# Sketch attention and mixture of experts on one core: k's load in front of S2's, a shorter chain of word operations, shared copies, 1e-6 by a product, and q pieces moved by one place

## The chip, the cores and the metric

One core of a Trainium2 chip. The metric is the device time of one execution in microseconds (us). The profiled span is some 1.8 us shorter than the device time of the same execution (489.55 and 491.35 us in the kernel before). In the views, PE is TensorE's matmuls, PEld its weight loads, DVE VectorE, ACT ScalarE, POOL GpSimd and SP SyncE; a pass is one matmul instruction, and a unit is the group of tokens whose queries are handled together.

## The reference, cut to what matters

```python
# q, k, v: (4, 4, 1088, 32); S1, S2: (8, 32) float64
def phi(x):                        # 64 features: products of two 8-wide projections
    a = einsum('rd,bhsd->bhsr', S1, x); b = einsum('rd,bhsd->bhsr', S2, x)
    return einsum('bhsi,bhsj->bhsij', a, b).reshape(..., 64)
kv  = einsum('bhsf,bhsd->bhfd', phi(k), v);  z = sum(phi(k), axis=s)
num = einsum('bhsf,bhfd->bhsd', phi(q), kv)
den = einsum('bhsf,bhf->bhs',  phi(q), z)[..., None] + 1e-06
x   = (num / den) as (4352, 128)
for e in range(4):                 # dense mixture of experts, D = 128, F = 1024
    out += p[:, e:e+1] * (relu(x @ w1[e]) @ w2[e])
```

S1 and S2 arrive as float64, two 32-bit words for each number. The kernel builds float32 from the words with integer operations on VectorE.

## The kernel before

The opening: loads on SyncE's and ACT's queues, warm-up matmuls, and the words of S. In the traces VectorE's operations of the opening start in the order of the program: in the changed kernel k had landed at 4.55 us, but its transpose, which stands behind the words, started at 6.58.

```python
s_raw = ...                                   # 16 x 64 int32: S1 over S2
for i, (eng, src) in enumerate(((nc.scalar, S1), (nc.sync, S2))):
    eng.dma_start(s_raw[R * i : R * i + R, :], src.bitcast(I32))
...
load_rows(k, 0, "kn")                         # 544 KB, SyncE's queue
load_rows(q, 0, "qn", slice(0, P))            # 64 KB
vn[0] = load_v(0)
...                                           # dp, ends, rest of q, w1 and w2 of each expert
keep_warm(10)                                 # 10 bf16 matmuls of 512 columns on zeros
# --- cut: thirteen word operations, a product, a transpose into s_T on VectorE ---
for h in range(H):
    nc.scalar.copy(<sk block h>, <s_T>)       # 4 on ACT
for i in range(3):
    nc.gpsimd.tensor_copy(<sp i>, <s_T>)      # 3 on POOL
for h in range(H):
    nc.gpsimd.tensor_copy(<sr block h>, <sp>) # 4 on POOL
# start(): transpose k (kT) and q; k projections kT x sk on TensorE; q's by sr;
#   products kp, qp; sums f over tokens; kvz; den and num; 1/den; xT; MoE begins
```

In the first unit 1e-6 is added on VectorE between den's transpose and the reciprocal. The later units run as small pieces between the MoE steps, one piece at each `yield`:

```python
def queries(b, c, n):
    qT = query_turn(b, c, n)                  # transpose on VectorE
    yield; yield; yield
    both(qc, sq, qT)                          # q projection on TensorE
    ...                                       # shuffles, sums, products qp on VectorE
    yield; yield
    yield from attend(...)                    # den products on TensorE, divide, transpose

def attend(...):
    for t in range(T[0]):                     # token tiles
        for p in range(2):                    # feature pairs
            for _ in range(2): on_side(nd[...], qp[p][:, at:at+64], kvx[b][:, p, :])
```

Of the kernel before, what the change touches and what calls it, by code (L numbers as in the profile page):

```python
# [8 lines left out]
F32 = mybir.dt.float32  # L9
# [14 lines left out]
def kernel(  # L24
# [58 lines left out]
    def psum(pool, tag):  # L83
        return pool.tile([P, 512], F32, tag=tag, name=tag)


    def load_rows(src, b, name, part=slice(0, S)):

        d = kn if name == "kn" else qn
        if b not in d:  # L90
            d[b] = lpool.tile([P, S], F32, tag=name, bufs=2, name=name)
        c, n = part.start, part.stop - part.start
        nc.sync.dma_start(d[b][:, part], bass.AP(src.tensor, src.offset + b * H * S * D + c, [[G * D, P], [1, n]]))
# [21 lines left out]
        load_rows(q, b, "qn")  # L115

    s_raw = cpool.tile([R2, 2 * D], I32, name="s_raw")
    for i, (eng, src) in enumerate(((nc.scalar, S1), (nc.sync, S2))):
        eng.dma_start(s_raw[R * i : R * i + R, :], src.bitcast(I32))  # L119
    w1_sb = cpool.tile([P, E, F], F32, name="w1_sb")  # L120
# [5 lines left out]
    def load_w2(e):  # L126
        nc.sync.dma_start(w2_sb[:, e], w2[e].rearrange("(f p) d -> p f d", p=P))

    load_rows(k, 0, "kn")
    load_rows(q, 0, "qn", slice(0, P))  # L130
    vn[0] = load_v(0)

# [36 lines left out]
    for h in range(H):  # L169
        nc.gpsimd.memset(own2[32 * h : 32 * h + 32, h % 2 : h % 2 + 1], 1.0)  # L170

    def keep_warm(n):

        for _ in range(n):
            wp = psum(ps_h, "h")
            nc.tensor.matmul(wp[:, :], warm[:, 0:P], warm[:, :], start=True, stop=True)  # L176

    keep_warm(10)


    turn = [0]
# [17 lines left out]
    def bits(out, in0, s1, op0, s2=None, op1=ALU.bypass):  # L199
        nc.vector.tensor_scalar(out=out, in0=in0, scalar1=s1, scalar2=s2, op0=op0, op1=op1)  # L200

    def either(out, a, b):
        nc.vector.tensor_tensor(out=out, in0=a, in1=b, op=ALU.bitwise_or)

    low = _ap(s_raw, 0, R2, 0, [[2, D]])
    high = _ap(s_raw, 0, R2, 1, [[2, D]])
# [5 lines left out]
    nc.vector.memset(s_hl[:, :], 0.0)  # L212
    bits(s_f[:, hi], high, 1, shl, 21, shr)
    bits(s_m[:, lo], high, 31, shr, 31, shl)

    bits(s_e[:, hi], s_f[:, hi], float(127 - 1023), ALU.add, 0.0, ALU.max)
    bits(s_e[:, lo], s_f[:, hi], float(127 - 1023 - 52), ALU.add, 0.0, ALU.max)
    bits(s_x[:, hi], high, 12, shl, 9, shr)
    bits(s_x[:, lo], low, 29, shr)
    bits(s_n[:, hi], s_e[:, hi], 1.0, ALU.min)  # L220
    bits(s_n[:, lo], low, 3, shl, 3, shr)
    bits(s_f[:, :], s_e[:, :], 255.0, ALU.min)
    either(s_x[:, hi], s_x[:, hi], s_x[:, lo])
    bits(s_e[:, :], s_f[:, :], 23, shl)
    either(s_m[:, hi], s_x[:, hi], s_m[:, lo])
    either(s_f[:, :], s_e[:, :], s_m[:, :])
    nc.vector.tensor_tensor(out=s_hl[0:R2, :], in0=s_n[:, :], in1=s_f[:, :].bitcast(F32), op=ALU.mult)
    nc.vector.transpose(s_T[:, :], s_hl[:, :])




    for h in range(H):
        nc.scalar.copy(_ap(sk, 32 * h, 32, R2 * h, [[HP, 2], [1, R2]]), _ap(s_T, 0, 32, 0, [[D, 2], [1, R2]]))
    for i in range(3):
        nc.gpsimd.tensor_copy(
            _ap(sp, 0, 32, HP * i, [[32, 2], [R, 4], [1, R]]),
            _ap(s_T, 0, 32, 4 * (i - 1) if i else R, [[D, 2]] + ([[1, 4], [0, R]] if i else [[0, 4], [1, R]])),
        )
    for h in range(H):  # L240
        nc.gpsimd.tensor_copy(
            _ap(sr, 32 * h, 32, 32 * h, [[P, 6], [1, 32]]), _ap(sp, 0, 32, 0, [[32, 6], [1, 32]])
        )
    mask_lo = [R2 + l % R2 for l in range(32)]
    mask_b = [R + l % R for l in range(32)]
    mask_a = [[4 * x + l // R for l in range(32)] for x in range(2)]
# [210 lines left out]
    def attend_first(b, c, n, qp):  # L457


        nd = [psum(ps_n, "den"), psum(ps_n, "num")]  # L460
        for i in range(2):
            for _ in range(2):
                on_side(
                    lambda s: nd[i][half[s], 0:n],
                    lambda s: kvzs[b][:, s, 1 - i, :],
                    lambda s: qp[s][:, 0:n],
                    start=True,
                    stop=True,
                )
        yield  # L470
        dT = apool.tile([P, UNITS[0][1]], F32, tag="dT", name="dT")
        nc.vector.transpose(dT[:, 0:n], nd[0][:, 0:n])
        yield
        rc = apool.tile([P, QW // 32], F32, tag="rc", name="rc")
        nc.vector.tensor_scalar(
            out=rc[:, 0 : n // 32], in0=_ap(dT, 0, P, 0, [[32, n // 32]]), scalar1=1e-6, scalar2=1.0, op0=ALU.add, op1=ALU.mult
        )
        nc.vector.reciprocal(rc[:, 0 : n // 32], rc[:, 0 : n // 32])
        rb = apool.tile([P, UNITS[0][1]], F32, tag="rb", name="rb")
        nc.vector.transpose(  # L480
            _ap(rb, 0, P, 0, [[32, n // 32], [1, 32]]), _ap(rc, 0, P, 0, [[1, n // 32], [0, 32]])
        )
        yield

        order = [[1, 4], [4, 32]] if c == 0 else [[32, n // 32], [1, 32]]
        nc.vector.tensor_tensor(  # L486
            out=_ap(xT, 0, P, c, order),
            in0=nd[1][:, 0:n].rearrange("p (g j) -> p g j", j=32),
            in1=rb[:, 0:n].rearrange("p (g j) -> p g j", j=32),
            op=ALU.mult,  # L490
        )
        have[0] += n
        yield

    def attend(b, c, n, qp):



        nd = [psum(ps_n, "den"), psum(ps_n, "num")]
        W = H * (D + 1)  # L500
        tiles = 0
        laid = []
        for c0, m in unit_parts(b, c, n):
            T = blocks(m)
            for t in range(T[0]):
                for p in range(2):
                    for _ in range(2):

                        at = c0 + P * t + (HP * turn[0] if t < T[turn[0]] else 0)
                        i, k = divmod(tiles + t, 3)  # L510
                        on_side(
                            lambda s: nd[i][half[s], W * k + W // 2 * p : W * k + W // 2 * (p + 1)],
                            lambda s: qp[p][:, at : at + HP],
                            lambda s: kvx[b][:, p, :],
                            start=True,
                            stop=True,
                        )
            laid.append((c0, T, tiles))
            tiles += T[0]
        yield  # L520
        banks = [(i, 3 * i, min(tiles, 3 * i + 3)) for i in range((tiles + 2) // 3)]
        rc = apool.tile([P, QW // 32], F32, tag="rc", name="rc")
        for i, t0, t1 in banks:
            nc.vector.tensor_scalar(
                out=rc[:, H * t0 : H * t1],
                in0=_ap(nd[i], 0, P, D, [[D + 1, H * (t1 - t0)]]),
                scalar1=1e-6, scalar2=1.0, op0=ALU.add, op1=ALU.mult,
            )
        nc.vector.reciprocal(rc[:, 0 : H * tiles], rc[:, 0 : H * tiles])
        yield  # L530
        xs = apool.tile([P, QW], F32, tag="qa", name="xs")
        for i, t0, t1 in banks:
            nc.vector.tensor_tensor(
                out=_ap(xs, 0, P, P * t0, [[D, H * (t1 - t0)], [1, D]]),
                in0=_ap(nd[i], 0, P, 0, [[D + 1, H * (t1 - t0)], [1, D]]),
                in1=_ap(rc, 0, P, H * t0, [[1, H * (t1 - t0)], [0, D]]),
                op=ALU.mult,
            )
        yield
        y = apool.tile([P, QW], F32, tag="y", name="y")  # L540
        for c0, T, t0 in laid:
            nc.vector.transpose(
                _ap(y, 0, P, P * t0, [[32, T[0]], [32 * T[0], H], [1, 32]]),
                _ap(xs, 0, P, P * t0, [[P, T[0]], [D, H], [1, D]]),
            )
            m = 64 * sum(T)
            base = xd.offset + P * (S * b + c + c0)
            for a in range(4):
                run = 32 * T[a // 2]
                nc.sync.dma_start(  # L550
                    bass.AP(
                        xd.tensor,
                        base + a // 2 * 64 * T[0] + a % 2 * run,
                        [[m, 32], [32 * m, H], [1, run]],
                    ),
                    _ap(y, 32 * a, 32, P * t0, [[32 * T[0], H], [1, run]]),
                )
            nc.sync.dma_start(
                xT[:, S * b + c + c0 : S * b + c + c0 + m],
                bass.AP(xd.tensor, base, [[m, P], [1, m]]),  # L560
            )
        have[0] += n
        yield

    def queries(b, c, n):
        qT = query_turn(b, c, n)
        yield
        yield
        yield
        qc = psum(ps_f, "f")  # L570
        both(qc[:, 0:n], sq[:, :], qT[:, 0:n], start=True, stop=True)
        yield
# [9 lines left out]
        for x in range(2):  # L582
            qa = apool.tile([P, QW], F32, tag="qa", name="qa")
            nc.vector.stream_shuffle(in_=qf[:, 0:n], out=qa[:, 0:n], mask=mask_a[x])  # L584
            yield
            for p in range(2):
                query_product(qp, p, x, n, qa, qb)
                yield
        yield
        yield  # L590
        yield from (attend_first if b == 0 and c < START[2] else attend)(b, c, n, qp)
# [357 lines left out]
```

## Time and profile before

| | kernel before |
|---|---|
| device time, median of 3 first runs | 491.51 us (491.39 to 491.71) |
| span of the profiled execution | 489.55 us |
| first useful matmul (k projection) | 5.82 us |
| from there to kvz on VectorE, "the block" | 5.84 us |
| kvz to the first MoE matmul, which starts at 14.16 us | 2.50 us |
| from there to the end, "the stretch" | 475.38 us |

The last four rows add up to the span (489.54). All later comparisons use these four stages, read from the start times in the trace. One row of the timeline (start, duration, what, idle time before it and what ended that):

```profile
1.19 3.86 PE L176 MATMUL h<-warm 128*128 128x512 bf16 x10 [1.19 <-DVE s_hl L212]
```

Ten warm-up matmuls run from 1.19 to 5.05. The first start 0.427 us apart, the last two 0.217: the trace's clock records put the change to full speed at 4.33 us. Before that the records are silent, so the clock column of a windows view shows 1.00 there although the pitch of 0.427 us is twice the later one; "half speed" below is meant so. ("Full speed from" below is the start of the first clock record in the packed trace; no view of `prof` prints it.)

### The profile page before, as it was taken

To read this page: it belongs to the slowest core of one execution; us is meant where nothing else is said; L and a number is where in the kernel's file an instruction comes from. 1 tells how busy PE (TensorE), PEld (TensorE's weight loads), DVE (VectorE), ACT (ScalarE), POOL (GpSimd) and SP (SyncE) were. 2 spreads that over 40 slices of the span, in tenths; PEclk is the share of its full clock that TensorE was granted. 3 is DMA by queue.
4 is the path that set the end of the run, shared out by engine and by line. 5 is a ranking of instruction groups with operands and counts; after the bars stand their busy time and mean duration, and the time that the engine had idled before them with its cause. 6 is when DMAs were issued, how large, how long until landed. Compare 5 with 4: busy or idle time off the path is not lost.

```text
span 489.5 us, 11439 instructions
## 1 busy us (share of the span) xinstructions
PE 482.6 (99%) x4602; PEld 361.1 (74%) x4602; DVE 318.5 (65%) x746; ACT 244.4 (50%) x487; POOL 226.8 (46%) x260
## 2 busy tenths in 40 slices
PE   8999999999999999999999999999999999999997
PEld 5877777777767777555777777777777777878997
DVE  6759585868676757768675564575575666665642
ACT  3344463455445634535455464445455455566651
POOL 6052473516355444334555353444555355555570
PEclk9999999999999999999999999999999999999999
DMA  7990230040102520041102200031101200120000
GB/s 207 290 284 22 88 95 1 2 137 1 34 2 80 139 55 1 1 118 23 33 2 87 50 0 1 2 87 23 33 1 55 49 1 1 50 50 2 15 3 18
DMA packets 37588, 26.25 MB, mean 54 GB/s; under 512 B 26016, under 2 KB 34592, under 8 KB 37024
## 3 DMA queue, kind: packets, MB, share of 16 engines
q1 hardware_dynamic: 37520, 25.53, 19.0%
q8 instruction: 36, 0.59, 0.5%
q14 instruction: 16, 0.13, 0.1%
q10 hardware_dynamic: 16, 0.00, 0.0%
HBM read 21.28 MB, written 4.24 MB: 52 GB/s over the span
## 4 chain that ended last, share of the span: by engine, by line
PE 96%; DVE 2%; DMA 1%; issue 0%; ACT 0%; SPq 0%; DVEq 0%
PE h L188 49%; PE o L188 40%; PE f L188 4%; PE den L188 3%; DMA kn<-in_k_dram 1%; DVE qp L450 1%; DVE hid L698 1%; PE num L188 1%; PE h L176 0%; DVE kT L314 0%; ACT hid L723 0%; DVE qa L584 0%; ACT sh L842 0%; SPq L119 0%; DVE xT L486 0%
## 5 line engine op out<-in xcount | busy, mean ns | idle before, releaser
L188 PE MATMUL h<-xT,w_sb 128*64 128x512 f32 (+4 forms) x1408 | 300.2, 495 | 0.5 <-DVE xT L486 0.5
L698 DVE SCALAR_TENSOR_TENSOR hid<-h,hid 128x256 f32<-128x256 f32 (+6 forms) x432 | 203.6, 472 | 148.2 <-ACT hid L723 139.2
L723 ACT ACTIVATE hid<-h 128x512 f32<-128x512 f32 (+3 forms) x288 | 158.4, 550 | 195.0 <-PE h L188 157.0
L188 PE MATMUL o<-hid,w2s 128*64 128x256 f32 (+3 forms) x1152 | 221.6, 355 | 0.0
L188 PE MATMUL o<-hid,w_sb 128*64 128x256 f32 (+3 forms) x864 | 183.9, 355 | 0.0
L188 PEld LDWEIGHTS h<-xT,w_sb 128*64 128x64 f32 x1408 | 144.2, 137 | 51.8 <-issue 9.2
L188 PEld LDWEIGHTS o<-hid,w2s 128*64 128x64 f32 x1152 | 131.7, 137 | 30.9 <-issue 0.2
L838 POOL TENSOR_TENSOR ev<-yz,sh 64x256 f32<-64x256 f32 (+3 forms) x72 | 48.4, 672 | 163.5 <-ACT sh L841 160.8
L188 PEld LDWEIGHTS o<-hid,w_sb 128*64 128x64 f32 x864 | 101.0, 137 | 24.5 <-issue 6.3
L826 POOL TENSOR_TENSOR yz<-ev 128x512 f32<-128x512 f32 (+3 forms) x36 | 42.1, 1170 | 61.8 <-ACT ev L829 61.8
L838 POOL TENSOR_TENSOR ct<-ev 128x512 f32<-128x512 f32 (+3 forms) x36 | 42.0, 1167 | 2.8
L838 POOL TENSOR_TENSOR ct<-ct,gate 128x512 f32<-128x512 f32 (+3 forms) x27 | 32.1, 1189 | 2.1
L838 POOL TENSOR_TENSOR total<-total,ct 128x512 f32<-128x512 f32 (+3 forms) x27 | 31.8, 1179 | 2.1
L450 DVE TENSOR_TENSOR qp<-qa,qb 64x384 f32<-64x384 f32 (+3 forms) x44 | 32.1, 729 | 1.0
L828 ACT COPY ev<-o 128x512 f32<-128x512 f32 (+3 forms) x36 | 19.4, 539 | 11.3 <-PE o L188 10.8
L188 PE MATMUL o<-w_sb,hid 128*64 128x128 f32 x256 | 21.7, 273 | 0.0
L829 ACT COPY ev<-o 128x512 f32<-128x512 f32 (+3 forms) x36 | 19.4, 539 | 2.6
L715 ACT ACTIVATE hid<-h 128x256 f32<-128x256 f32 x24 | 9.2, 384 | 21.2 <-PE h L188 20.7
L188 PEld LDWEIGHTS o<-w_sb,hid 128*64 128x64 f32 x256 | 17.8, 137 | 2.1 <-issue 1.9
L353 DVE TENSOR_TENSOR kp<-fs 128x256 f32<-128x256 f32 (+1 forms) x24 | 14.7, 617 | 0.0
L841 ACT COPY sh<-yz 64x256 f32<-64x256 f32 (+3 forms) x36 | 13.7, 379 | 1.7 <-POOL yz L826 0.8
L842 ACT COPY sh<-yz 64x256 f32<-64x256 f32 (+3 forms) x36 | 13.7, 380 | 0.9
(113 smaller groups left out, 230.2 us busy)
## 6 DMA issues: line engine op xcount, KB each, us to landing
w_sb<-in_moe_w_dram SPq DMA_DIRECT2D x8, 512.0 KB, 7.5
gate<-gates SPq DMA_DIRECT2D x4, 1024.0 KB, 5.5
kn<-in_k_dram SPq DMA_DIRECT2D x4, 544.0 KB, 4.6
vn<-in_v_dram SPq DMA_DIRECT2D x16, 128.0 KB, 4.2
gate<-gates SPq DMA_DIRECT2D x2, 896.0 KB, 5.7
qn<-in_q_dram SPq DMA_DIRECT2D x3, 544.0 KB, 5.5
xd<-y SPq DMA_DIRECT2D x26, 48.0 KB, 1.7
out_dram<-ob SPq DMA_DIRECT2D x16, 64.0 KB, 2.0
```

Of the source, the lines that this page charges most:

```text
L188: nc.tensor.matmul(out(s), weights(s), moving(s), **flags)
L353: eng.tensor_tensor(out=_ap(kps[b], 0, P, 256 * t0 + P * p + 64 * x, [[256, n], [32, 2], [R, 4], [1, R]]), in0=_ap(src, 0, P, off + 4 * x, ...
L450: nc.vector.tensor_tensor(out=qp[p][64 * x : 64 * x + 64, 0:n], in0=qa[64 * p : 64 * p + 64, 0:n], in1=qb[64 * p : 64 * p + 64, 0:n], op=A ...
L698: nc.vector.scalar_tensor_tensor(out=out, in0=src, scalar=0.0, in1=in1, op0=ALU.max, op1=ALU.subtract)
L715: nc.scalar.activation(hd[:, 0 : 2 * n], hp[:, 0 : 2 * n], ACTF.Relu)
L723: nc.scalar.activation(hd[:, n * j : n * j + n], hp[:, 0:n], ACTF.Relu)
L826: add = lambda out, in0, in1, op=ALU.add: nc.gpsimd.tensor_tensor(out=out, in0=in0, in1=in1, op=op)
L828: nc.scalar.copy(_ap(ev, 0, P, 0, [[2 * w, 2], [1, w]]), _ap(a0, 0, P, 0, two))
L829: nc.scalar.copy(_ap(ev, 0, P, w, [[2 * w, 2], [1, w]]), _ap(a1, 0, P, 0, two))
L838: add = lambda out, in0, in1, op=ALU.add: nc.gpsimd.tensor_tensor(out=out, in0=in0, in1=in1, op=op)
L841: nc.scalar.copy(sh[HP:P, 0:w], yz[0:HP, 0, 0:w])
L842: nc.scalar.copy(sh[0:HP, 0:w], yz[HP:P, 1, 0:w])
```

## The change

Its intent: let k's load, which the chain waits for, start 0.47 us earlier; shorten the word operations and the copies behind them, so that they don't become the bound; take one addition off the first division; keep TensorE from waiting for qp in the later units. Cut to its core:

```diff
     s_raw = cpool.tile([R2, 2 * D], I32, name="s_raw")
+    load_rows(k, 0, "kn")
     for i, (eng, src) in enumerate(((nc.scalar, S1), (nc.sync, S2))):
         eng.dma_start(s_raw[R * i : R * i + R, :], src.bitcast(I32))
...
-    load_rows(k, 0, "kn")
     load_rows(q, 0, "qn", slice(0, P))
...
+    eps = ...            # one row of 1e-6, the rest 0
-    keep_warm(10)
+    keep_warm(8)
...                       # OR with a shift in one operation; two operations fewer
-        nc.vector.tensor_tensor(out=out, in0=a, in1=b, op=ALU.bitwise_or)
+        nc.vector.scalar_tensor_tensor(out=out, in0=in0, scalar=s1, in1=in1, op0=op0, op1=ALU.bitwise_or)
...                       # copies of S: sk 2 on ACT, 2 on POOL; sp 2 on POOL, 1 on ACT; sr 2 and 2
+        if c == 0:        # first unit: den starts as ones x eps
+            for _ in range(2):
+                on_side(<nd[0] half>, <ones of vx>, <eps>, start=True, stop=False)
...                       # and its addition of 1e-6 on VectorE goes
-            for t in range(T[0]):
-                for p in range(2):
+            for p in range(2):
+                for t in range(T[0]):
...
         qT = query_turn(b, c, n)
         yield
         yield
-        yield
         qc = psum(ps_f, "f")
...
+        yield             # one more before the den products
         yield
         yield
```

More of the change, by code (lines that the diff above doesn't have):

```diff
@@ L170 @@
         nc.gpsimd.memset(own2[32 * h : 32 * h + 32, h % 2 : h % 2 + 1], 1.0)
+    eps = cpool.tile([P, 1], F32, name="eps")
+    nc.gpsimd.memset(eps[:, :], 0.0)
+    nc.gpsimd.memset(eps[0:1, :], 1e-6)
     def keep_warm(n):
@@ L200, in bits, with either @@
         nc.vector.tensor_scalar(out=out, in0=in0, scalar1=s1, scalar2=s2, op0=op0, op1=op1)
-    def either(out, a, b):
-        nc.vector.tensor_tensor(out=out, in0=a, in1=b, op=ALU.bitwise_or)
+    def either(out, in0, s1, op0, in1):
+        nc.vector.scalar_tensor_tensor(out=out, in0=in0, scalar=s1, in1=in1, op0=op0, op1=ALU.bitwise_or)
     low = _ap(s_raw, 0, R2, 0, [[2, D]])
@@ L214, with copy_on @@
     bits(s_m[:, lo], high, 31, shr, 31, shl)
+    bits(s_x[:, hi], high, 12, shl, 9, shr)
     bits(s_e[:, hi], s_f[:, hi], float(127 - 1023), ALU.add, 0.0, ALU.max)
     bits(s_e[:, lo], s_f[:, hi], float(127 - 1023 - 52), ALU.add, 0.0, ALU.max)
-    bits(s_x[:, hi], high, 12, shl, 9, shr)
-    bits(s_x[:, lo], low, 29, shr)
-    bits(s_n[:, hi], s_e[:, hi], 1.0, ALU.min)
+    either(s_x[:, hi], low, 29, shr, s_x[:, hi])
     bits(s_n[:, lo], low, 3, shl, 3, shr)
     bits(s_f[:, :], s_e[:, :], 255.0, ALU.min)
-    either(s_x[:, hi], s_x[:, hi], s_x[:, lo])
-    bits(s_e[:, :], s_f[:, :], 23, shl)
-    either(s_m[:, hi], s_x[:, hi], s_m[:, lo])
-    either(s_f[:, :], s_e[:, :], s_m[:, :])
+    either(s_m[:, hi], s_m[:, lo], 0, shl, s_x[:, hi])
+    bits(s_n[:, hi], s_e[:, hi], 1.0, ALU.min)
+    either(s_f[:, :], s_f[:, :], 23, shl, s_m[:, :])
     nc.vector.tensor_tensor(out=s_hl[0:R2, :], in0=s_n[:, :], in1=s_f[:, :].bitcast(F32), op=ALU.mult)
     nc.vector.transpose(s_T[:, :], s_hl[:, :])
+    def copy_on(scalar):
+        return nc.scalar.copy if scalar else nc.gpsimd.tensor_copy
     for h in range(H):
-        nc.scalar.copy(_ap(sk, 32 * h, 32, R2 * h, [[HP, 2], [1, R2]]), _ap(s_T, 0, 32, 0, [[D, 2], [1, R2]]))
+        copy_on(h < 2)(_ap(sk, 32 * h, 32, R2 * h, [[HP, 2], [1, R2]]), _ap(s_T, 0, 32, 0, [[D, 2], [1, R2]]))
     for i in range(3):
-        nc.gpsimd.tensor_copy(
+        copy_on(i == 2)(
             _ap(sp, 0, 32, HP * i, [[32, 2], [R, 4], [1, R]]),
@@ L240 @@
     for h in range(H):
-        nc.gpsimd.tensor_copy(
-            _ap(sr, 32 * h, 32, 32 * h, [[P, 6], [1, 32]]), _ap(sp, 0, 32, 0, [[32, 6], [1, 32]])
-        )
+        copy_on(h > 1)(_ap(sr, 32 * h, 32, 32 * h, [[P, 6], [1, 32]]), _ap(sp, 0, 32, 0, [[32, 6], [1, 32]]))
     mask_lo = [R2 + l % R2 for l in range(32)]
@@ L460, in attend_first @@
         nd = [psum(ps_n, "den"), psum(ps_n, "num")]
+        if c == 0:
+            for _ in range(2):
+                on_side(
+                    lambda s: nd[0][half[s], 0:n],
+                    lambda s: _ap(vx, 0, P, D, [[0, HP]]),
+                    lambda s: _ap(eps, 0, P, 0, [[0, n]]),
+                    start=True,
+                    stop=False,
+                )
         for i in range(2):
@@ L466, in attend_first @@
                     lambda s: qp[s][:, 0:n],
-                    start=True,
+                    start=(i > 0 or c > 0),
                     stop=True,
@@ L474, in attend_first @@
         rc = apool.tile([P, QW // 32], F32, tag="rc", name="rc")
-        nc.vector.tensor_scalar(
-            out=rc[:, 0 : n // 32], in0=_ap(dT, 0, P, 0, [[32, n // 32]]), scalar1=1e-6, scalar2=1.0, op0=ALU.add, op1=ALU.mult
-        )
-        nc.vector.reciprocal(rc[:, 0 : n // 32], rc[:, 0 : n // 32])
+        column = _ap(dT, 0, P, 0, [[32, n // 32]])
+        if c:
+            nc.vector.tensor_scalar(
+                out=rc[:, 0 : n // 32], in0=column, scalar1=1e-6, scalar2=1.0, op0=ALU.add, op1=ALU.mult
+            )
+            column = rc[:, 0 : n // 32]
+        nc.vector.reciprocal(rc[:, 0 : n // 32], column)
         rb = apool.tile([P, UNITS[0][1]], F32, tag="rb", name="rb")
```

## The prediction

> **What bounds the kernel now.** I read the page's engine shares first, then the windows of the stages, then the chain of waits and the timeline of the first 15 us, then the list of DMA issues of that stretch, and last every wait of TensorE. The windows (us; busy time and instructions of PE, PEld, DVE, ACT, POOL; granted clock, DMA share, GB/s):
>
> ```profile
> PE 482.6 (99%) x4602; PEld 361.1 (74%) x4602; DVE 318.5 (65%) x746; ACT 244.4 (50%) x487; POOL 226.8 (46%) x260
> ...
> 0.00:5.82 5.82, 3.86 (x11) 1.29 (x11) 3.06 (x19) 2.35 (x6) 3.37 (x20) 1.00 0.61 170
> 5.82:11.55 5.73, 5.73 (x168) 5.59 (x168) 4.06 (x15) 2.25 (x7) 4.23 (x15) 1.00 0.89 234
> 11.55:14.16 2.61, 1.63 (x12) 0.75 (x13) 1.95 (x9) 0.00 (x0) 0.39 (x2) 1.00 1.05 350
> 26.00:486.00 460.00, 459.39 (x4229) 342.84 (x4225) 299.48 (x679) 235.48 (x463) 218.43 (x224) 1.00 0.16 43
> 486.00:489.50 3.50, 0.15 (x3) 0.00 (x0) 0.35 (x1) 0.00 (x0) 0.00 (x0) 0.93 0.07 21
> ```
>
> From 14.16 us to 486 TensorE never rests but for 0.61 us. What can be won without removing matmul work is therefore the opening (no useful matmul before 5.82, no MoE matmul before 14.16), that one stall, and the 3.5 us tail, which the change doesn't touch. The chain of waits through the opening (start, duration, what):
>
> ```profile
> 0.74 0.41 SPq L119
> 1.21 3.73 DMA kn<-in_k_dram
> 4.96 0.72 DVE kT L314
> 5.82 2.32 PE h L188 x72
> 9.45 2.12 PE f L188 x72
> 13.68 0.40 DVE xT L486
> ```
>
> So the end is set by: S2's issue, k's load, k's transpose on VectorE, then 5.73 us of unbroken TensorE work, then a short VectorE chain to the first xT. The S words run beside k's load, as the timeline shows (start, duration, what, idle time before it and its end):
>
> ```profile
> 2.47 0.17 DVE L200 TENSOR_SCALAR s_f<-s_raw 16x32 int32<-16x32 int32 x1 [1.27 <-DMA s_raw<-in_S_dram]
> ...
> 4.21 0.23 DVE L228 STREAM_TRANSPOSE s_T<-s_hl 32x64 f32<-32x64 f32 x1
> ...
> 4.96 1.30 DVE L314 STREAM_TRANSPOSE kT<-kn 128x512 f32<-128x512 f32 x2 [0.52 <-DMA kn<-in_k_dram]
> ```
>
> The words end at 4.44 and VectorE then idles 0.52 us for k: they have half a microsecond of slack, no more. How transfers share SyncE's queue is in the DMA issues of the first 9 us (KB each, us from issue to landing):
>
> ```profile
> kn<-in_k_dram SPq DMA_DIRECT2D x1, 544.0 KB, 3.7
> ...
> qn<-in_q_dram SPq DMA_DIRECT2D x1, 64.0 KB, 3.6
> ```
>
> The 64 KB behind k were issued at 1.62 and landed at 5.20, 0.26 us after k (4.94). In the packet records none of its 512-byte packets starts before 4.14[...]. S2's 2 KB, issued in front of k at 0.74, were used at 2.47.
>
> [...] Here the 512-column warm-up matmuls start 0.427 us apart until 4.16 and 0.216 apart from 4.46, and the last window's clock of 0.93 is half speed from 489.0 on, 2.9 us after the last matmul. [...]
>
> **Part 1, k's load in front of S2's.** k is issued at 0.74 instead of 1.21, so it lands about 0.47 earlier, at 4.46. If only k mattered this would be the gain. But S2 now stands behind k's 544 KB: it lands with k, near 4.45, not near 2.4. In the kernel before, S2's last completion write was at 2.00 and the first word operation at 2.47; the same 0.47 behind a completion write near 4.03 puts that operation at 4.50, that is 2.03 us later. [...] the words stand in front of k's transposes. **This is the decisive step.**
>
> **Part 2, twelve word operations.** Before, fourteen and a transpose take 2.47 to 4.44, 1.97 us. The pitches in the trace are 0.09 for an independent operation, about 0.2 to 0.25 for each of the last ones that read the operation just before. After: ten at 0.09 are 0.9, the last OR waits a little (0.04), then OR to product 0.247, product to transpose 0.246, transpose 0.232: 1.67 us, so 0.30 saved. The words end near 4.50 + 1.67 = 6.17.
>
> **Part 3, k's transposes and the copies of S.** k's first transpose can then start at 6.10 (successors start about 0.07 before the end of an independent predecessor, as the two kT ones do) instead of 4.96; it takes 0.71, and 0.146 later, as before, TensorE starts: 6.96 instead of 5.82, **+1.14 us**. The copies of sk, two on ACT (0.22 each) and two on POOL instead of four on ACT, end near 6.7 and just stay off the path; without the sharing they would end at 7.15 and cost another 0.3. sr is not needed until 2.06 us into TensorE's work.
>
> **Part 4, 1e-6 by a product.** Removed from the path: the addition before the reciprocal, 12.85 to 13.05, **-0.20 us**. Added: four matmul passes of 128 columns, about 0.067 each (sixteen such take 1.07), 0.27 us. They stand between the last f matmul and the first den one, where TensorE waits 0.46 us for kvz; hidden. The words on VectorE that made k late also move fs, kp and qp by the same 1.14; v's landing (7.67), which ACT waited 0.39 for, no longer binds.
>
> **Part 5, the later units.** The one stall: 24 den products at 199.2, of which four start and the rest wait for qp:
>
> ```profile
> 198.66 1.63 DVE L450 TENSOR_TENSOR qp<-qa,qb 64x384 f32<-64x384 f32 x1
> ...
> 200.34 0.67 PEld L188 LDWEIGHTS den<-kvx,qp 128*64 128x64 f32 x20 [0.74 <-DVE qp L450]
> ```
>
> Starts of TensorE there are 0.83 us apart instead of 0.04. I counted through the pacing of the pieces as the source sets it: taking a pause before the q projection away and adding one before the products leaves the total at 19 pieces, so the products stay put and every piece between comes one place, mostly half a step, earlier. The last qp then ends before the products are due, and pair by pair ordering covers 12 passes instead of 4 in any wait left: **-0.8 us**. The price: the q projection comes up to one h pair (0.86 us) earlier, while its transpose ended only 0.55 (unit at 104) and 0.54 (at 210) before it was used. Two stalls of about 0.3: **+0.6 us**. In the other units the slack is 1.9 or more, or the move is small. Matmul counts don't change, so this part is about -0.2.
>
> **Part 6, two warm-up matmuls fewer.** Eight end by 4.6. With TensorE's start at 6.96 it idles about 2.4 us, against 0.77 before. [...]
>
> **Sum:** +1.14 - 0.20 - 0.2 + 0.4 = +1.14, so 491.51 + 1.14, about **492.7 us**.
>
> **The rivals.** (A) S2 does not wait for k's packets, and k's lead counts: TensorE starts at about 5.4, -0.45, with -0.2 from the addition and -0.2 later: 490.7. For it: the packet of a small transfer needs only 15 to 18 ns of an engine. Against it: the 64 KB behind k, all of whose packets waited. I give it one in eight. (B) S2 waits, but the clock stays open: 492.2. (C) S2 waits and the clock closes [...] in most runs: 493.5 to 494. (D) The earlier q pieces make more stalls than I counted, or delay hid products so that TensorE waits for a bank; each would show as 0.3 to 1 us, adding 1 or so to any of these. (E) The products gain more by the new order than the one stall; against it, all other den groups start their passes about 0.04 apart already.
>
> **Range and chances.** The cases run from 490.7 (A) to 494 (C with D). Weighted, eight in ten lie in 491.0 to 494.2. Two per cent are 9.8 us; no term here is near that: within 2% 0.985, faster 0.005, slower 0.01.
>
> **What would show it.** Right: the first word operation waits for S's DMA until about 4.5; the words take near 1.7 us; k's first transpose starts near 6.1 with no wait for k; the first sk,kT matmul is near 7.0 and the first MoE matmul near 15.1; no addition before the first reciprocal; no wait for qp near 200. Wrong: s_f still near 2.5 to 2.9 (then rival A); warm-up or sk,kT matmuls at a 0.07 us pitch well past 7 (then C); waits of den or f for qT or qp of over 1 us in sum (then D).

Passages that rest on rules which no trace showed are cut. Among them are the grounds of part 6 and its term of +0.4 us for TensorE's clock, an estimate that was not worked out from a trace. The sum, which came to +1.14 us and 492.7 us, still holds that term; the terms left come to +0.74, that is 492.25 us, rival B's 492.2. The 493.5 to 494 of rival C rests on the same cut estimate. That S2 would wait behind k was read from the 64 KB behind k, none of whose packets started before 4.14 us and which landed 0.26 us after k.

## The result, and the profile after

The changed kernel took 494.99 us in the median of 6 runs (493.71 to 495.59), beside 491.70 for the kernel before (491.39 to 493.85, 6 runs). The ratio is 1.0056, with a 95% interval of 1.0032 to 1.0079. Ratios here are the mean time of one kernel's fast runs over that of the other's of the same rounds, so not quite the ratio of the medians. The change is within 2%, but the time lies above the predicted range (491.0 to 494.2). The profiled execution took 495.59 us, the slowest of the six. One of the six runs of the kernel before took 493.85, some 2 us more than the other five; it has no profile.

Engine shares, then windows of the four stages (us; busy time and instructions of PE, PEld, DVE, ACT, POOL; granted clock, DMA share, GB/s):

```profile
PE 486.0 (98%) x4604; PEld 354.6 (72%) x4604; DVE 315.1 (64%) x743; ACT 245.4 (50%) x488; POOL 227.3 (46%) x261
...
0.00:7.39 7.39, 3.60 (x9) 1.08 (x9) 2.66 (x17) 2.10 (x5) 2.87 (x20) 1.00 0.67 170
7.39:15.80 8.41, 8.41 (x172) 8.25 (x172) 4.16 (x16) 3.16 (x10) 4.84 (x17) 1.00 0.98 302
15.80:18.09 2.29, 1.71 (x14) 0.75 (x13) 1.77 (x8) 0.00 (x0) 0.00 (x0) 1.00 1.08 353
18.09:490.30 472.21, 472.18 (x4412) 344.55 (x4412) 306.19 (x705) 240.10 (x474) 219.61 (x225) 1.00 0.17 46
```

The block that took 5.73 us of unbroken TensorE work with 168 passes now takes 8.41 with 172, and TensorE is as busy in it as before. It isn't waiting; it is slow. The chain of waits through the opening:

```profile
0.74 0.40 SPq L93
1.20 3.70 DMA s_raw<-in_S_dram
4.99 0.17 DVE s_f L205
...
6.42 0.23 DVE s_T L232
6.65 0.60 DVE kT L319
7.39 4.11 PE h L193 x72
...
13.56 2.14 PE f L193 x72
```

The DMA in the chain is now S2's, not k's. The 72 k projections take 4.11 us instead of 2.32; the 72 sums f, later, take 2.14 as before (2.12). The timeline shows the wait and the warm-up:

```profile
1.19 3.60 PE L181 MATMUL h<-warm 128*128 128x512 bf16 x8 [1.19 <-DVE s_hl L218]
4.99 0.17 DVE L205 TENSOR_SCALAR s_f<-s_raw 16x32 int32<-16x32 int32 x1 [3.80 <-DMA s_raw<-in_S_dram]
...
6.58 1.25 DVE L319 STREAM_TRANSPOSE kT<-kn 128x512 f32<-128x512 f32 x2
7.39 1.87 PE L193 MATMUL h<-sk,kT 128*64 128x64 f32 x30 [2.60 <-DVE kT L319]
```

VectorE idles 3.80 us for S2 and not at all for k. In the packet records S2's eight 256-byte packets start at 3.57 to 3.98; k landed at 4.55. In the clock records full speed begins at 12.92 us, so TensorE worked from 7.39 to 12.92, 5.53 us, at half speed.

| stage | before | after | difference | my term |
|---|---|---|---|---|
| to the first k projection | 5.82 | 7.39 | +1.57 | +1.14 |
| block, to kvz | 5.84 | 8.41 | +2.57 | +0.4 |
| kvz to MoE | 2.50 | 2.29 | -0.21 | -0.20 |
| stretch | 475.38 | 475.72 | +0.34 | -0.2 |
| span | 489.55 | 493.81 | +4.26 | +1.14 |

### The profile page after: what moved, and what is told of

It reads as the page before. It is cut to its first block, busy times and chain, and to the rows that moved or that the text cites. A ratio compares the mean times of both kernels' runs of the same rounds, so it can differ in the third digit from the quotient of the medians.

```text
span 493.8 us, 11442 instructions
## 1 busy us (share of the span) xinstructions
PE 486.0 (98%) x4604; PEld 354.6 (72%) x4604; DVE 315.1 (64%) x743; ACT 245.4 (50%) x488; POOL 227.3 (46%) x261
## 4 chain that ended last, share of the span: by engine, by line
PE 98%; DMA 1%; DVE 1%; issue 0%; SPq 0%; DVEq 0%
PE h L193 50%; PE o L193 41%; PE f L193 4%; PE den L193 3%; DMA s_raw<-in_S_dram 1%; PE num L193 1%; PE h L181 0%; DVE kT L319 0%; SPq L93 0%; DVE end L779 0%; DVE kvz L381 0%; DVE s_f L205 0%; DVE s_T L232 0%; DVE s_hl L231 0%; DVE s_n L205 0%
## 5 line engine op out<-in xcount | busy, mean ns | idle before, releaser
L193 PE MATMUL o<-hid,w2s 128*64 128x256 f32 (+3 forms) x1152 | 217.3, 355 | 0.0
L193 PEld LDWEIGHTS o<-hid,w2s 128*64 128x64 f32 x1152 | 129.8, 137 | 41.0 <-issue 9.2
L455 DVE TENSOR_TENSOR qp<-qa,qb 64x384 f32<-64x384 f32 (+3 forms) x44 | 28.5, 649 | 1.1
L193 PE MATMUL o<-w_sb,hid 128*64 128x128 f32 x256 | 24.1, 273 | 0.0
L193 PEld LDWEIGHTS o<-w_sb,hid 128*64 128x64 f32 x256 | 20.1, 137 | 2.0 <-issue 1.6
```

The source lines that it names most:

```text
L193: nc.tensor.matmul(out(s), weights(s), moving(s), **flags)
L455: nc.vector.tensor_tensor(out=qp[p][64 * x : 64 * x + 64, 0:n], in0=qa[64 * p : 64 * p + 64, 0:n], in1=qb[64 * p : 64 * p + 64, 0:n], op=A ...
```

## The experiments

Theory: S2, queued behind k's 544 KB, delays the words and TensorE's start; the long rest of TensorE, with fewer warm-up matmuls, leaves its clock at half speed for a time that differs between executions. Rivals: the block is slow because its operands come late; the other parts of the change cost the time; eight warm-up matmuls are too few whatever S2 does; S2's later issue, not the bytes in front of it, is the delay. Every kernel below gave correct results.

### S2's load back in front, all else of the change kept: s2_first

```diff
-    load_rows(k, 0, "kn")
     for i, (eng, src) in enumerate(((nc.scalar, S1), (nc.sync, S2))):
         eng.dma_start(...)
+    load_rows(k, 0, "kn")
```

> The changed kernel with S2's load put back in front of k's; everything else of the change stays, eight warm-up matmuls too. Theory (S2 waits in SyncE's queue behind k, and the long rest of TensorE that follows keeps its clock at half): the first word operation is back near 2.47 us, the words end near 4.15, TensorE starts sk,kT near 5.8, and the rest before it is only about 1.2 us, so that the block of 172 passes takes 5.7 us [...], not 8.4; MoE begins near 14.0; time near 491.5. Rival (eight warm-up matmuls are too few for the clock whatever S2 does): TensorE starts near 5.8 but its block still takes over 7 us; time near 493.5. Rival (S's place matters nothing): unchanged at 495.

491.59 us (491.23 to 493.42, 4 runs), ratio 1.0006 (0.9986 to 1.0025). The timeline:

```profile
2.50 0.18 DVE L205 TENSOR_SCALAR s_f<-s_raw 16x32 int32<-16x32 int32 x1 [1.30 <-DMA s_raw<-in_S_dram]
...
5.37 1.31 DVE L319 STREAM_TRANSPOSE kT<-kn 128x512 f32<-128x512 f32 x2 [1.21 <-DMA kn<-in_k_dram]
6.23 2.32 PE L193 MATMUL h<-sk,kT 128*64 128x64 f32 x72 [1.44 <-DVE kT L319]
```

The words are back at 2.50, k is the bound again, and the block takes 5.84 us with eight warm-up matmuls (full speed from 5.18). One line moved undoes the loss. Eight warm-up matmuls sufficed in this execution; the one run of 493.42 suggests that they don't in every execution, but it has no profile.

### More warm-up, S2 still behind k: warm14

```diff
-    keep_warm(8)
+    keep_warm(14)
```

> The changed kernel with 14 warm-up matmuls instead of 8; S2 still behind k. Theory: S2's wait is untouched (first word operation near 5.0, TensorE's first sk,kT matmul near 7.4), but the clock is open by then and the block of 172 passes takes 5.73 us, not 8.36: MoE begins near 15.5 instead of 18.1, time near 493.0. Rival (the block is slow because its operands come late, vx, fs or sr, not because of the clock): the block still takes over 8 us, time near 495.

492.29 us (491.80 to 492.63), ratio 1.0011 (0.9997 to 1.0026). Windows of the opening:

```profile
0.00:6.60 6.60, 5.41 (x14) 1.85 (x14) 2.82 (x17) 2.16 (x5) 3.02 (x21) 1.00 0.65 186
6.60:12.48 5.88, 5.88 (x173) 5.71 (x172) 3.91 (x16) 2.96 (x9) 4.45 (x16) 1.00 0.76 225
```

The block is back to 5.87 us by the start times (5.88 between the window's rounded ends) with S2 still late (first word operation at 4.04, TensorE's start at 6.60). Its operands and passes are those of the changed kernel; only the matmuls in front differ. That refutes late operands. The time is 0.7 under the one that I expected; in the profile S2 came at 4.04, not near 5.0.

### S2 on ACT's queue, k first on SyncE's: s2_on_act

```diff
-    ... enumerate(((nc.scalar, S1), (nc.sync, S2))):
+    ... enumerate(((nc.scalar, S1), (nc.scalar, S2))):
-    keep_warm(8)
+    keep_warm(10)
```

> The changed kernel with S2's load on ACT's queue behind S1's, so that k is first on SyncE's queue and S2 is behind nothing large; ten warm-up matmuls as in the kernel before. Theory: S2 lands near 2.6 to 2.9, the words end near 4.6, k at 4.55, TensorE starts near 5.4, MoE begins near 13.5; time 0.4 to 0.8 under the kernel before, 490.9 to 491.4. Rival ([...] S2 waits for k's packets on either queue): the words start near 5.0 as in the changed kernel, time 493 to 495.

493.34 us (491.83 to 493.93), ratio 1.0023 (1.0004 to 1.0042). My theory missed; the rival held.

```profile
4.63 0.17 DVE L205 TENSOR_SCALAR s_f<-s_raw 16x32 int32<-16x32 int32 x1 [3.43 <-DMA s_raw<-in_S_dram]
```

S1's packets, issued at 0.74 on the same queue, start at 1.70 to 1.79; S2's, issued at 1.35, at 3.64 to 3.88, when nearly all of k's are through (the last k packet starts at 3.81). So in this run the other queue did not bring S2 past a load that had been issued 0.6 us before it.

### The kernel before with the one load moved: only_k_first

```diff
 # kernel before
+    load_rows(k, 0, "kn")
     for i, (eng, src) in enumerate(((nc.scalar, S1), (nc.sync, S2))):
...
-    load_rows(k, 0, "kn")
     load_rows(q, 0, "qn", slice(0, P))
```

> The kernel before with k's load in front of S2's and nothing else of the change: fourteen word operations, ten warm-up matmuls, all copies of sk on ACT. Theory: first word operation near 5.0, words end near 6.95, sk's copies near 7.95, TensorE starts near 8.0 (2.2 later than before); ten warm-up matmuls end near 5.45, a rest of about 2.5 us[...]; time 493.7 to 496. Rival (the loss comes of the other parts of the change, mainly eight warm-up matmuls): time within 0.5 of the kernel before.

494.19 us (492.41 to 495.09), ratio 1.0047 (1.0023 to 1.0070). The loss comes with this one move, with ten warm-up matmuls and none of the other parts. From the chain of waits of the profiled execution, which took 492.41 us, the fastest of the four:

```profile
1.20 2.71 DMA s_raw<-in_S_dram
4.01 0.17 DVE s_f L200
...
7.07 2.32 PE h L188 x72
```

S2 came at 4.01 here, 1.0 earlier than I expected, and TensorE started at 7.07, not 8.0. The clock opened at 5.26, so the block took 5.84. This execution shows S2's wait without the clock's share. The other three runs (493.62 to 495.09) have no profile, so that the clock made them longer is not shown. It does show what the old copies of sk cost: from the words' end to TensorE's start it takes 1.09 us with four copies on ACT, the last of which releases TensorE, and 0.74 in the changed kernel.

### S2 behind 64 KB instead of 544: s2_behind_q

```diff
+    load_rows(q, 0, "qn", slice(0, P))
     for i, (eng, src) in ...: eng.dma_start(...)
+    load_rows(k, 0, "kn")          # both moved from their old places; and 10 warm-up matmuls
```

> The changed kernel with q's 64 KB first on SyncE's queue, then S2, then k, ten warm-up matmuls: S2 is issued as late as in the changed kernel (near 1.20), but behind 64 KB instead of 544. Theory (the bytes in front of it are what S2 waits for): first word operation near 3.0 us; words end near 4.7, k lands near 5.4 and is the bound again, TensorE starts near 6.2. Rival (the later issue and the queue's fixed time make the delay, whatever stands in front): first word operation at 4.0 to 5.0 as in the other runs with S2 second.

492.98 us (2 runs, 491.89 and 494.06), ratio 1.0028 (1.0006 to 1.0050).

```profile
2.89 0.20 DVE L205 TENSOR_SCALAR s_f<-s_raw 16x32 int32<-16x32 int32 x1 [1.69 <-DMA s_raw<-in_S_dram]
...
6.36 1.30 DVE L319 STREAM_TRANSPOSE kT<-kn 128x512 f32<-128x512 f32 x2 [1.82 <-DMA kn<-in_k_dram]
```

S2 was issued at 1.20, as late as in the changed kernel, but was used at 2.89 instead of 4.0 to 5.3. So the bytes in front of it are what it waits for. k, now third, landed at 6.33, nearly a microsecond later than I expected, and was the bound; the block took 7.10 us (full speed from 9.99).

### The clock alone: s2f_warm1

```diff
 # s2_first
-    keep_warm(8)
+    keep_warm(1)
```

> The changed kernel with S2 in front of k, but one warm-up matmul instead of eight: the clock by itself, without S2's wait. Theory: words and k as with S2 in front (2.5 and about 5.0), TensorE starts near 5.9, and the block from there to kvz takes 7.4 to 8.5 us instead of 5.84 [...]; time 492.5 to 494.5. Rival (the block was slow in the changed kernel for another reason than the clock): 5.84 us, time 491.5.

492.40 us (492.36 to 492.85), ratio 1.0019 (1.0003 to 1.0034). S2 and k are as in s2_first, TensorE starts at 5.88, and the block is slow again; the windows view of the block:

```profile
5.88:13.04 7.16, 7.16 (x172) 7.00 (x172) 4.07 (x16) 2.25 (x7) 3.92 (x13) 1.00 0.95 260
```

The clock opens at 8.78. The time just misses the expected range from below; the block of 7.16 us just misses its own, too.

### The changed kernel again: after_again

No edit.

> The changed kernel once more, unaltered[...]. Theory: first word operation again at 4.0 to 5.0; the block from TensorE's start to kvz takes between 5.84 and 8.5 us and follows from where the clock opens in the trace[...]. Rival: the block takes 8.4 us again whatever the clock.

494.56 and 494.38 us, ratio 1.0058. The windows of the same three opening stages:

```profile
0.00:7.67 7.67, 3.60 (x9) 1.07 (x9) 2.66 (x17) 2.10 (x5) 2.85 (x20) 1.00 0.63 164
7.67:14.72 7.05, 7.05 (x172) 6.89 (x172) 4.07 (x16) 3.02 (x10) 4.81 (x17) 1.00 0.96 306
14.72:17.01 2.29, 1.71 (x14) 0.75 (x13) 1.77 (x8) 0.00 (x0) 0.00 (x0) 1.00 1.12 340
```

The same program's block took 7.05 us instead of 8.41, with S2 still later (5.28). What differs is where the clock opened: 10.32 instead of 12.92. One part of the expectation, how busy TensorE must be before the clock opens, missed (0.77 against over 0.80; part 6 below has the estimate). In the profiles of the opening's experiments the block follows from where the clock opened:

| kernel | TensorE starts | full speed from | block | over 5.84 | half of the time at half speed |
|---|---|---|---|---|---|
| before | 5.82 | 4.33 | 5.84 | 0 | 0 |
| s2_first | 6.23 | 5.18 | 5.84 | 0 | 0 |
| only_k_first | 7.07 | 5.26 | 5.84 | 0 | 0 |
| warm14 | 6.60 | 5.86 | 5.87 | 0.03 | 0 |
| s2f_warm1 | 5.88 | 8.78 | 7.16 | 1.32 | 1.45 |
| s2_behind_q | 7.22 | 9.99 | 7.10 | 1.26 | 1.39 |
| after_again | 7.67 | 10.32 | 7.05 | 1.21 | 1.33 |
| s2_on_act | 7.03 | 10.41 | 7.38 | 1.54 | 1.69 |
| after | 7.39 | 12.92 | 8.41 | 2.57 | 2.77 |

The last column is half of (full speed from, less start): at half speed, as in the warm-up's pitches of 0.427 and 0.217 us, a time t holds the work of t/2. It exceeds the loss by 0.12 to 0.20 us in every slow row. Of the seven profiles that follow, six had full speed before TensorE's start and a block of 5.84; in w10_b it came at 6.08, after a start at 5.94, and the block took 5.9.

### The rest of the change without its first part: w10, w10_b

```diff
 # s2_first
-    keep_warm(8)
+    keep_warm(10)
```

> The changed kernel with S2's load in front of k's and ten warm-up matmuls, that is: the rest of the change without its first part. Theory (all of the loss came of the queue and the clock): opening as in the kernel before less the addition; MoE begins 13.9 to 14.2, the stretch from there to the end 475.4, as in the other run with S2 in front (475.41); time within 0.5 of the kernel before, 491.2 to 491.8. Rival (the later units cost something too): the stretch after MoE's start is 0.3 to 0.5 longer than the 475.38 of the kernel before, time 491.8 to 492.2.

491.48 us (491.12 to 492.10), ratio 0.9997 (0.9982 to 1.0012). The stretch was 475.85 in this profile, so the rival looked right. A second set of five runs, beside a twin with the old pauses:

> w10 once more, with more rounds, on the same chip as its twin with the old pauses. Stretch after MoE's start 475.3 to 475.9 as in the six profiles with the new pauses (475.30 to 475.85); time 491.2 to 491.8, equal to the kernel before within 0.1 per cent.

491.45 us (491.10 to 491.84), ratio 0.9998 (0.9985 to 1.0012), stretch 475.37. The stretch scatters by half a microsecond for one program, mostly between 92 and 120 us after MoE's start; one profile doesn't decide between 475.4 and 475.8. As a whole the rest of the change is worth nothing that these runs can tell.

### The old pauses: w10_old_pauses, w10_old_pauses_b

```diff
 # w10
         qT = query_turn(b, c, n)
         yield
         yield
+        yield
...
-        yield             # the third one before the products
```

> As w10, but with the pauses as in the kernel before (three ahead of the q projection, two ahead of the products). Theory (my step in the prediction): the q projections at 104 and 210 no longer wait for the transpose (0.25 and 0.17 gained), but the products near 199 wait again for qp; pair by pair order covers twelve passes, so that the stall is about 0.55 instead of 0.83. Stretch after MoE's start 475.4 to 475.7. Rival (the pauses are worth nothing, the order alone took the stall away): no stall near 199, stretch 475.0 to 475.2.

490.95 us (490.73 to 491.76), ratio 0.9988 (0.9973 to 1.0003). The stretch, 475.55, is in the expected range. The stall near 199 is back, with twelve passes ahead of it instead of four; the starts of TensorE there are 0.59 us apart, 0.55 was expected (timeline):

```profile
199.89 0.77 PE L193 MATMUL den<-kvx,qp 128*64 128x66 f32 x12
...
201.03 0.57 PE L193 MATMUL den<-kvx,qp 128*64 128x66 f32 x12 [0.37 <-DVE qp L455]
```

> w10_old_pauses once more with more rounds. If the new pauses cost as much as they save (part 5 of the prediction off by its whole 0.2), its time equals w10_b's within 0.2 us and its stretch after MoE's start lies inside the other's range. If they cost more than they save, as 490.95 against 491.48 suggests, it is again about 0.5 us under w10_b and 0.1 per cent under the kernel before.

491.33 us (491.24 to 491.60), ratio 0.9996 (0.9984 to 1.0009), stretch 475.29. The half microsecond of the first set didn't return. This is the fastest version tried, but both intervals take in 1: it isn't shown to beat the kernel before.

### The old order of the products: w10_old_order

```diff
 # w10
-            for p in range(2):
-                for t in range(T[0]):
+            for t in range(T[0]):
+                for p in range(2):
```

> As w10, but the products token pair by token pair as in the kernel before, with the new pauses. Theory (the pauses alone take the stall near 199 away, and the new order costs about 0.17 in some groups, as the 1.07 against 0.90 from first to last start at 121 and 260 suggest): no stall near 199, first to last start back to 0.90, stretch after MoE's start 0.3 to 0.5 shorter than in w10, 474.9 to 475.1. Rival (the order covers the stall): a wait for qp near 199, stretch 475.6 or more.

491.36 us (491.22 to 492.00), ratio 0.9998. No wait for qp near 199, so the pauses alone remove the stall. The first-to-last starts of the groups at 121 and 260 stayed at 1.07, so the order isn't what costs there, and the stretch (475.48) is inside w10's scatter. My second guess fell: with the new pauses the order is worth nothing either way.

### 1e-6 added on VectorE again: w10_old_eps

```diff
 # w10: eps products out, start=True for den, addition in front of the reciprocal for every unit
```

> As w10, but 1e-6 added on VectorE again in the first unit, no product. Theory: from kvz's start to MoE's start takes 2.50 us as in the kernel before instead of 2.29 as in the changed one: 0.2 us more, all of it on the path. Rival (the four added passes stand in front of the den products and take what they save): the same 2.3.

491.44 us (491.21 to 491.80), ratio 0.9996. kvz to MoE takes 2.50 us, as in the kernel before; the profiles with the product have 2.29 or 2.30, except two (w10 and w10_old_pauses, 2.46 and 2.45) in which the first w1 load landed only at 14.03 and 14.29, after xT was ready. So the product saves 0.20 us unless the weights are late.

### Three pauses in both places: pauses33

```diff
 # w10
+        yield             # three before the q projection, three before the products
-            count, columns = count + 19, columns + n
+            count, columns = count + 20, columns + n
```

> S2 in front, ten warm-up matmuls, the rest of the change, and three pauses both ahead of the q projection and ahead of the products (twenty pieces a unit, and the count that paces them set to twenty): the q projection should not wait for its transpose (0.25 and 0.17 less than in w10), nor the products for qp (0.6 to 0.8 less than with the old pauses). Theory: stretch after MoE's start 474.6 to 475.0, time 490.6 to 491.0, some 0.15 per cent under the kernel before. Rival (denser pieces delay VectorE's hid products elsewhere): stretch 475.4 or more, time as w10.

491.54 us (491.08 to 491.68, 5 runs), ratio 0.9996 (0.9984 to 1.0009), stretch 475.50. The rival held. The q projection near 105 still waits for its transpose (0.63 us at its weight load), and the stretch is no shorter. That the denser pacing, which moves all pieces, is the reason was not tested.

## Why the prediction was wrong

**Part 1, S2 behind k: right in kind, short by half a microsecond.** S2's last data packet started at 3.98, close to what was worked out (a completion write near 4.03). But I put the first word operation 0.47 us after that write, as in the kernel before. Behind k it came 1.02 us after the packet's start, at 4.99. Over all profiles this gap is 0.41 to 0.65 with S2 in front of k and 0.65 to 1.16 behind it. The semaphore records in the traces narrow it down: S2's completion is counted in eight increments, and the first word operation starts 0.10 us after the last of them. In only_k_first and warm14 all eight had come by 3.91 and 3.94. In the changed kernel seven had come by 4.44 and the last came at 4.89; in after_again six by 4.23 and the other two at 5.05 and 5.18. So one or two of eight increments make the latest cases. Why these come late stays open. k itself landed 0.39 earlier, not 0.47, which bound nothing.

**Part 2, the words: right.** They took 4.99 to 6.65, 1.66 us; 1.67 was predicted. A shift with OR in one operation took 0.17 us for 16x32 integers, 0.10 to the next operation (5.43 to 5.53); in the kernel before the OR alone took 0.17 and 0.11 (3.29 to 3.40). With S2 in front they have slack again (1.2 us of waiting for k in s2_first), so that this saving reaches the end only where S2 is late.

**Part 3: right apart from what part 1 passed on.** k's first transpose started with no wait at 6.58, 0.07 before the words' end, TensorE at 7.39: +1.57 instead of +1.14. The 0.43 is the late S2 (0.49), less 0.05 by which the way from the transpose to TensorE was shorter. That the shared copies save 0.3 was not tested alone; only_k_first, without them, needs 0.35 more from the words' end to TensorE.

**Part 4: right.** -0.21 measured. The timeline of the changed kernel:

```profile
15.48 0.40 PE L193 MATMUL den<-eps,vx 128*64 128x128 f32 x4
...
16.14 0.44 PE L193 MATMUL den<-qp,kvz 128*64 128x128 f32 x4 [0.26 <-DVE kvz L381]
...
16.98 0.18 DVE L495 RECIPROCAL rc<-dT 128x4 f32<-128x4 f32 x1
```

The four passes end before kvz is there, TensorE still waits 0.26 us, and no addition stands in front of the reciprocal.

**Part 5: the stall went, its price was larger than thought.** The wait for qp near 199 is gone in all profiles with the new pauses. From 183 to 192 us after MoE's start s2_first gains 0.99 us on the kernel before. The q projections near 104 and 210 do wait, as worked out:

```profile
108.13 0.20 PEld L193 LDWEIGHTS f<-qT,sq 128*64 128x64 f32 x4 [0.91 <-DVE qT L448]
```

They cost 0.25 and 0.16. Some further shifts of 0.15 to 0.2 that I hadn't counted, two in the first 45 us after MoE's start and one near 245, use up the rest. Net: +0.03 in s2_first, +0.34 in the changed kernel's profile, with a scatter of that size; -0.2 was predicted. What makes the uncounted shifts wasn't settled: no matmul waits at them. At the first, near 10 us after MoE's start, a weight load waits 0.34 us for qp (at 23.91 in s2_first), which none does there in the kernel before; it was not tested alone.

**Part 6, the step that failed: the clock.** The term was +0.4, the estimate above. It measured +2.57 and +1.21 in two profiles of the changed kernel. I took it that the warm-up opens the clock near 4.33 as before, and asked in the sum only whether the rest closes it again (rival C does name a late opening). The runs showed the opposite order: in both profiles of the changed kernel the warm-up never opened the clock. It opened at 12.92 and 10.32 us, long after the warm-up's end. In all 16 profiles the time from the clock's opening to its closing is either 484.69 or 481.28 us; the two differ by 3.41 us and are about 142 and 141 times that. My estimate from these figures is that in these runs the clock changed only at points 3.41 us apart. Counted back from 12.92, the stretches between them in the profiled execution were 2.68 to 6.09, 6.09 to 9.50 and 9.50 to 12.92. Estimated from the starts of the matmuls, TensorE was busy for 0.56 and 0.61 of the first two, the first cut by the end of warm-up at 4.6, the second by the start at 7.39; the third was full of k's matmuls, and at its end the clock opened. By the same estimate the stretch in front of the opening was filled to 0.77 in after_again (6.91 to 10.32, TensorE's start at 7.67) and to 0.81 in s2_behind_q, and the fullest one without an opening to 0.70 (s2_on_act, 0.18 to 3.59, warm-up from 1.19). That the filling is the cause was not tested by itself. So the profiled block ran 5.5 us at half speed. The two profiles with S2 behind k in which the clock opened before TensorE's start (only_k_first at 5.26, warm14 at 5.86) lost 0 and 0.03 us. The place of the opening would also explain why the changed kernel's runs spread over 1.9 us, but runs without a profile can't show it.

**Rivals.** A (S2 doesn't wait) is refuted by every run with S2 behind k. C (the clock) is what came, larger than sized. D's waits for qT came: at the weight loads they are 0.91, 0.83 and 0.29 in s2_first, 2.0 us in sum and over the 1 us that I had named as the sign, but the two long ones moved TensorE by only 0.25 and 0.16. The change's share by parts: moving k's load alone has the ratio 1.0047, the changed kernel 1.0056, the rest without the move 0.9998.

## What to carry to other kernels

Before moving a big load ahead of a small one, ask who needs the small one first: here 2 KB paid for 544 KB, on either queue (first used at 4.99 us on SyncE's and 4.63 on ACT's, instead of 2.47), and the work that it fed stood in front of the big load's on the same engine, which took them in that order (k landed at 4.55, its transpose started at 6.58). A late start of TensorE can be paid twice: in both profiles of the changed kernel the first block began at half speed and took 2.57 and 1.21 us longer. Size that cost as half of the time from TensorE's start to full speed (5.53 and 2.65 us there; the loss was 0.12 to 0.20 us under the half in every slow profile), and take it as a lottery among runs: in only_k_first TensorE started nearly as late, at 7.07, and its block lost nothing. Let warm-up matmuls last until the first real one is ready, as in warm14, and count them after every change of the opening.
